# A two-layer decode step: bf16 turns of o and of row sums, a norm without helper tiles, another projection form, and a new written-out order

## The chip, the cores and the metric

The kernel runs on one core of a Trainium2 chip. A core has a matrix engine (TensorE, here PE, with its weight loads as PEld), a vector engine (DVE), a scalar engine (ACT), a general engine (POOL) and a queue engine (SP) that issues nearly all transfers. Each engine works off its own instructions in order; engines wait for each other by semaphores. Matrix products go to PSUM, eight banks of 128 partitions by 512 FP32 numbers; everything else lives in SBUF. The metric is the device time of the whole program in microseconds, lower is better.

## The reference

Four sequences (B = 4) with one token each pass through two identical layers. A layer is a windowed attention over a key/value cache and a gated feed-forward block, both with a norm ahead and a residual add behind:

```
x = x + attention(norm(x));  x = x + ffn(norm(x));  and the same once more

attention: q = x @ wq            (448 -> 16 heads of 256; 8 key/value heads, two q heads each)
           k, v = last 2048 positions of the caches, per sequence and key/value head
           p = softmax(q k^T / 16);  o = p v;  out = o @ wo      (4096 -> 448)
ffn:       (silu(x @ w_gate) * (x @ w_up)) @ w_down              (448 -> 1792 -> 448)
norm:      (x - mean) / sqrt(var + 1e-5)
```

Both layers use the same weights and the same caches. Inputs and output are bf16. A pair of one sequence and one key/value head reads 1 MB of keys and 1 MB of values; there are 32 such pairs per layer, 64 units of work in all.

## The kernel before, in words

The program is built as a graph of operations (`Graph`, `Op`), each with an engine, a short kind name and the data that it reads and writes. The order on every engine is not worked out at build time: it is written down as lists of operation numbers (`SEQ_PE`, `SEQ_DVE`, `SEQ_ACT`, `SEQ_POOL`, `SEQ_SP`), and `SLOTS` says into which of 34 SBUF units of 0.5 MB each load goes. `schedule` reads the lists and adds, for every load into a unit that is in use, a wait for the last reader of what lies there; `_place_waits` sets the semaphores. `DUR` holds estimated durations and only serves to sort the waits. Entries such as `w13` in `SEQ_PE` are fillers: products of zeros with 512 columns into bank A (`filler`, L1111–1114) that change no value and keep PE working; there are 317.

`PLAN` says in which stages the 64 units run and which are done two at a time (`+`) or with their scores one after the other (`&`). `HOLD` names the keys and values of layer 0 that stay in SBUF for layer 1. The last stages are `210+310`, `311` and `315+312`; a unit is written as sequence, layer, head.

A unit or pair of units (`group`, L831) goes through these steps. Its keys are transposed in place by DVE (L856, twice per unit). POOL spreads q over a block form `qe` (L896). PE forms the scores (L890), DVE takes the maximum (L906), PE spreads it (L911, L914), DVE negates it (L920), ACT takes the exponent (L924), PE turns the probabilities (L937), ACT copies them (L946), PE and DVE sum them (L954, L959), PE multiplies by the values (L968), and POOL inverts the sum (L981). The result o then lies in rows that have to be turned into columns. In all groups but the last this takes an ACT copy to bf16 (L995), a DVE subtraction (L997) that leaves the high and the low part of o as one bf16 tile, and two bf16 products (L1003). In the last group (`final`) ACT copies o as FP32 (L984) and two FP32 products turn it (L989). DVE scales it into `oT` (L1013).

The output projection (`out_proj`) has two forms. By rows (`opr`, L1033) four products per head add 4×448 results into rows of bank A. By columns (`opc`, L1025) sixteen products add 128-row columns into a corner of the same bank. The column form is used in the stage that ends a token's layer, the row form elsewhere. When a token's layer ends, `rows(t)` brings its row sums back to columns: ACT copies 448 FP32 numbers of bank A (L773), PE turns them with four FP32 products (L778; the trace counts two PE passes for each) and a product with zeros (`clear`, L529), and DVE adds them to x (L782). `residual` adds the column sums (L525).

`norm(t)` sums x and its square (L525, L538) on DVE, PE adds over the partitions and spreads the result (`nstat`, L541), DVE subtracts the mean (L545) and copies the sums (L547), and POOL works out the reciprocal root (L557–561). The width 448 is 3×128 + 64, so the last 64 rows of wq, gate and up are laid over 128 partitions as two half rows each. In before, row r of these lies in partitions 2r and 2r+1, and the last 64 values of x are spread to match by a PE product with a helper tile `twice` (L549) and a DVE product with a second one, `par` (L552), into spare columns of the statistics tile. `qproj` then forms q for a token (L595), scales it (L601), turns it (L611), copies it (L618) and selects head parts by sixteen products (L626). The feed-forward block has a column form (`ffn`, L720, L731, L734–747, L756) and a row form for tokens 1 and 2 of layer 0 (`ffn_row`, L657–685).

The queue order by which SP issues loads is fixed by `SEQ_SP`: first keys, x and wq, then keys and values mixed with wo, gate, up and down, and at the end two key halves and four value halves of the last group.

Of the kernel before, what the change touches and what calls it, by code (L numbers as in the profile page):

```python
# [5 lines left out]
ACT = mybir.ActivationFunctionType  # L6
# [4 lines left out]
INT32 = mybir.dt.int32  # L11
# [38 lines left out]
    "000 001 002 003 004 005 006 007 010 011 100 101 102 103 104 105 110 201 202 205 206 207 302 304 306 307 310 "  # L50
# [35 lines left out]
)  # L86
SEQ_DVE = (
# [21 lines left out]
)  # L109
SEQ_ACT = (  # L110
# [8 lines left out]
)  # L119
# [221 lines left out]
def build(nc, A_x, A_k_cache, A_v_cache, A_wq, A_wo, B_x, B_w_gate, B_w_up, B_w_down, out):  # L341
# [3 lines left out]
    with ExitStack() as es:  # L345
        def sb(name, shape, dt):
            return es.enter_context(nc.sbuf_tensor(name, shape, dt))
# [831 lines left out]
```

## Time and profile before

| | |
|---|---|
| time, median of 3 runs | 281.68 us (281.52 to 282.57) |
| the profiled execution | 281.3 us, its span 279.4 us |
| PE busy | 256.0 us (92%) |
| DVE busy | 179.5 us (64%) |
| POOL, ACT busy | 80.3 us, 61.8 us |
| read from memory | 103.91 MB, 372 GB/s over the span |
| granted PE clock, mean | 0.964 |

In what follows a row of a timeline has the start, the length, the engine, the line of the kernel, the operation and its operands (output `<-` input), and how many instructions were merged; in brackets stands how long the engine had been idle before and what it had waited for. A row of a group has the operands, the count, then the busy time of all and the mean time of one in ns, then the idle time ahead of them. A row of a stretch has the stretch, its length, and for each engine the busy time and the number of instructions, then the granted clock of PE, the share of the DMA engines and the rate. Products overlap on PE, so the mean time of one is longer than its share of a row of many.

### The profile page before, as it was taken

The page shows a single profiled execution, that of the slowest core. Times are in us where ns is not written, and L with a number is a line of the kernel's source. Part 1 is how long each engine was busy: PE and PEld are TensorE (multiplying, and loading weights), DVE is VectorE, ACT ScalarE, POOL GpSimd, SP SyncE. Part 2 cuts the span into 40 slices and gives each one's busy share as a digit, 9 for nine tenths or more (in the row PEclk, how much of TensorE's full clock was granted, in tenths as well). Part 3 has the DMA queues.
Part 4 walks back from the last instruction along what each step waited for, and adds up shares of the span by engine and source line. Part 5 has one row for each costly group of instructions (what it writes and reads, how often), then busy time and mean ns, then how long its engine had stood idle before and what let it go on. Part 6 is the DMA issues. An engine that isn't in the chain of part 4 may idle for free. (4 is left out here: it accounts for less than half of the span.)

```text
span 279.4 us, 10832 instructions
## 1 busy us (share of the span) xinstructions
PE 256.0 (92%) x4796; PEld 149.3 (53%) x4796; DVE 179.5 (64%) x548; ACT 61.8 (22%) x173; POOL 80.3 (29%) x225
## 2 busy tenths in 40 slices
PE   3899799999999999999998889999998999999995
PEld 1333344334775554545555445655764577576684
DVE  4388644634603789668766978793898858489421
ACT  0003010101113222232223123134213212423301
POOL 1033230011121534315232333243153242423430
PEclk9999989999999999999999999999999999989857
DMA  7999999999999999999999999999999999999200
GB/s 282 428 419 420 413 409 409 395 394 406 401 394 409 396 412 410 412 401 361 409 401 420 418 412 409 393 369 412 414 420 402 405 400 382 392 414 412 115 2 2
DMA packets 26894, 104.61 MB, mean 374 GB/s; under 512 B 2652, under 2 KB 6752, under 8 KB 22880
## 3 DMA queue, kind: packets, MB, share of 16 engines
q1 hardware_dynamic: 26839, 103.92, 93.5%
q8 instruction: 37, 0.61, 0.9%
q14 instruction: 10, 0.07, 0.1%
q10 hardware_dynamic: 8, 0.00, 0.0%
HBM read 103.91 MB, written 0.00 MB: 372 GB/s over the span
## 5 line engine op out<-in xcount | busy, mean ns | idle before, releaser
L856 DVE STREAM_TRANSPOSE half<-half 128x1024 uint32<-128x1024 uint32 x88 | 106.6, 1228 | 9.3 <-DMA half<-in_A_k_cache_dram 9.2
L1112 PE MATMUL A<-identb,small 128*128 128x512 bf16 x317 | 96.2, 399 | 4.4 <-DVE A L424 4.4
L981 POOL TENSOR_TENSOR small<-small 128x2 f32<-128x2 f32 (+1 forms) x48 | 38.5, 804 | 54.1 <-DVE small L959 54.1
L968 PE MATMUL Y<-half,pT 128*8 128x256 bf16 (+1 forms) x1024 | 45.7, 281 | 3.1 <-DMA half<-in_A_v_cache_dram 1.0
L890 PE MATMUL S<-half,qe 128*8 128x128 bf16 (+1 forms) x1536 | 43.5, 241 | 0.6 <-DVE half L856 0.2
L1112 PEld LDWEIGHTS A<-identb,small 128*128 128x128 bf16 x317 | 27.6, 104 | 29.9 <-issue 12.5
L890 PEld LDWEIGHTS S<-half,qe 128*8 128x8 bf16 x1536 | 30.8, 85 | 10.9 <-issue 1.6
L924 ACT ACTIVATE po<-S,small 104x128 bf16<-104x128 f32 (+1 forms) x48 | 19.3, 402 | 68.7 <-DVE small L920 66.6
L896 POOL TENSOR_TENSOR qe<-qc,tiny 128x64 bf16<-128x64 bf16 x64 | 17.9, 292 | 45.6 <-PE S L890 29.1
L997 DVE SCALAR_TENSOR_TENSOR po<-po,small,Y 128x256 bf16<-128x256 bf16 x47 | 22.0, 468 | 13.3 <-ACT po L995 13.2
L968 PEld LDWEIGHTS Y<-half,pT 128*8 128x8 bf16 (+1 forms) x1024 | 20.3, 85 | 17.6 <-issue 6.9
L995 ACT ACTIVATE po<-Y 128x256 bf16<-128x256 f32 x47 | 18.0, 383 | 48.1 <-PE Y L968 33.2
L906 DVE TENSOR_REDUCE tiny<-S 104x1 bf16<-104x128 f32 (+1 forms) x48 | 15.6, 326 | 11.5 <-PE S L890 11.2
L557 POOL TENSOR_SCALAR st<-st 128x1 f32<-128x1 f32 x16 | 4.2, 264 | 58.5 <-DVE st L547 52.5
L946 ACT ACTIVATE pT<-Y 128x64 bf16<-128x64 f32 (+1 forms) x48 | 12.2, 258 | 27.8 <-PE Y L937 27.7
L1033 PE MATMUL A<-wo_sb,oT 128*4 128x448 bf16 x188 | 16.4, 353 | 0.9 <-DVE oT L1013 0.9
L920 DVE TENSOR_REDUCE small<-S 104x1 f32<-104x32 f32 x48 | 8.6, 180 | 10.4 <-PE S L914 8.3
L1013 DVE TENSOR_TENSOR oT<-Y,small 128x4 bf16<-128x4 f32 (+1 forms) x63 | 8.9, 153 | 7.7 <-PE Y L989 4.6
L911 PE MATMUL S<-small,identb 104*104 104x32 bf16 x48 | 10.1, 210 | 3.4 <-DVE small L459 2.0
L1060 POOL MEMSET oT<- 128x16 bf16 x38 | 4.1, 111 | 29.9 <-PE A L1033 23.2
L959 DVE TENSOR_REDUCE small<-Y 128x2 f32<-128x32 f32 (+1 forms) x48 | 9.2, 191 | 5.0 <-PE Y L954 4.8
L778 PE MATMUL Z<-small,wide 128*128 128x1 f32 (+1 forms) x80 | 10.9, 249 | 0.5 <-ACT wide L773 0.5
(136 smaller groups left out, 268.0 us busy)
## 6 DMA issues: line engine op xcount, KB each, us to landing
half<-in_A_v_cache_dram SPq DMA_DIRECT2D x87, 512.0 KB, 10.6
half<-in_A_k_cache_dram SPq DMA_DIRECT2D x28, 1024.0 KB, 10.6
half<-in_A_k_cache_dram SPq DMA_DIRECT2D x32, 512.0 KB, 6.7
wo_sb<-in_A_wo_dram SPq DMA_DIRECT2D x8, 448.0 KB, 13.5
half<-in_A_wq_dram SPq DMA_DIRECT2D x3, 1024.0 KB, 12.3
wd_sb<-in_B_w_down_dram SPq DMA_DIRECT2D x1, 1568.0 KB, 20.2
wg_sb<-in_B_w_gate_dram SPq DMA_DIRECT2D x1, 1344.0 KB, 15.7
wu_sb<-in_B_w_up_dram SPq DMA_DIRECT2D x1, 1344.0 KB, 17.8
```

Source lines behind the costliest of these rows:

```text
L856: return e.transpose(a, a)
L890: last = e.matmul(Sb[s_][qd:qd + 8, 0:32 * 2 * J], lhsT=qe[q_][:, P, ce, :, :].rearrange("p a n -> p (a n)"), rhs=keys(kcs[P], J * x, J, c ...
L896: g.op(POOL, "qe", lambda e, P=P, t=t, kvh=kvh: e.tensor_tensor(qe[q_][:, P, :, :, :], qc[t][:, kvh, :, :].unsqueeze(2).broadcast_to([128, ...
L906: g.op(DVE, f"max{n}", lambda e: e.tensor_reduce(pmax[s_][0:R, :], Sb[s_][0:R, 0:N], AX.X, ALU.max), r=(f"s{s_}",), w=(f"pmax{s_}",), bank ...
L924: return e.activation(praw[0:R, 0:128 * n].rearrange("p (g r l) -> p g r l", g=2 * n, l=2), Sb[s_][0:R, 0:128 * n].rearrange("p (l g r) -> ...
L946: g.op(SCA, f"pt{n}", lambda e: e.activation(pf, Yb[p_][:, 0:PW], ACT.Copy), r=(f"yp{p_}",), w=(f"pT{pt}",), bank=(f"Y{p_}",))
L968: last = e.matmul(Yb[p_][32 * gg:32 * gg + M, 256:512], lhsT=pT[pt][:, gg, 2 * a + hv, 4 * P:4 * P + M] if n == 2 else p1[:, gg % 2, 2 * a ...
L981: g.op(POOL, f"pow{n}", lambda e: e.tensor_tensor(ri[p_][:, 0:2 * n], rs[p_][:, 0:2 * n], expo[:, 1:1 + 2 * n], op=ALU.pow), r=(f"rs{p_}", ...
L995: g.op(SCA, "oh", lambda e: e.activation(oh[:, :], Yb[p_][:, 256:512], ACT.Copy), r=(f"y{p_}",), w=("oh",), bank=(f"Y{p_}",))
L997: g.op(DVE, "oho", lambda e: e.scalar_tensor_tensor(out=oh[:, :], in0=oh[:, :], scalar=lomask[:, 0:1], in1=Yb[p_][:, 256:512], op0=ALU.mul ...
L1033: last = e.matmul(Ab[32 * k:32 * k + B, 0:D], lhsT=oT[oi][:, k % 2, k // 2, :], rhs=wo_sb[:, 4 * kvh + k, :], start=False, stop=False, ski ...
L1112: return e.matmul(Ab[:, 0:512], lhsT=zero[:, 0:1].broadcast_to([128, 128]), rhs=identb[:, :].unsqueeze(1).broadcast_to([128, 4, 128]), sta ...
```

## The change

- `rows(t)`: ACT copies the row sums as bf16, DVE subtracts that copy from the FP32 sums (a new instruction, `rowsub`) and so gets the rest as a second bf16 tile, and PE turns both with eight bf16 products after a product with zeros.
- The last group turns o like all others: ACT copy to bf16, DVE subtraction, two bf16 products. The FP32 form is gone.
- `norm` no longer uses `twice`, `par` and the PE product; two DVE instructions subtract the mean from the last 64 values and write them to the upper and the lower half of a tile `xe` of its own. The last rows of wq, gate and up are loaded to match: half h of row r goes to partition 64h + r.
- The projection of the second-last stage (`311`) is done by columns.
- The selection of q multiplies by a mask in the DVE copy and needs four products instead of sixteen; `tsel` is a view of the identity instead of a tile.
- The product with zeros (`clear`) comes first instead of last.
- All five order lists and `SLOTS` are new. The order of the loads is the same, but keys 001 and 201 (sequence, layer, head) come in two halves where they came in one piece, and keys 106 and 112 in one piece where they came in halves. There are 270 fillers for 317.

```diff
         def clear(e, out, m):
-            return e.matmul(out, lhsT=zero[:, 0:1].broadcast_to([128, 64]), rhs=identb[:, 0:m], start=False, stop=True,
-                            skip_group_check=True)
+            e.matmul(out, lhsT=zero[:, 0:1].broadcast_to([128, 64]), rhs=identb[:, 0:m], start=True, stop=False,
+                     skip_group_check=True)
...
-            vec("nxn", lambda e: e.tensor_scalar(xn[:, :, t], x[:, t, :], Z2[:, 0:1], None, op0=ALU.subtract),
+            vec("nxn", lambda e: e.tensor_scalar(xn[:, :, t], x[:, t, 0:3], Z2[:, 0:1], None, op0=ALU.subtract),
...
-            g.op(PE, "nxe", lambda e: e.matmul(Z2[:, 16:17], lhsT=twice[:, :],
-                                                    rhs=xn[:, 3, t:t + 1], start=True, stop=True, skip_group_check=True),
-                 r=(f"xn{t}", "twice"), w=("z2",), bank=("Z2",))
-            vec("nxe2", lambda e: e.tensor_tensor(xe[:, :, t], par[:, :], Z2[:, 16:17].broadcast_to([128, 2]), op=ALU.mult),
-                ("z2", "par"), (f"xe{t}",), ("Z2",))
+            for h in range(2):
+                vec(f"nx{1 + h}", lambda e, h=h: e.tensor_scalar(
+                    xe[64 * h:64 * h + 64, h, t:t + 1], x[64:128, t, 3:4], Z2[64:128, 0:1], None, op0=ALU.subtract),
+                    (f"x{t}", "z2"), (f"xe{t}",), ("Z2",))
...
         def rows(t):
-            g.op(SCA, "rowcp", lambda e: e.activation(wide[:, 0:D], Ab[:, 0:D], ACT.Copy), r=(f"row{t}",), w=WIDE, bank=("A",))
+            g.op(SCA, "rowcp", lambda e: e.activation(wideb[:, 0:D], Ab[:, 0:D], ACT.Copy), r=(f"row{t}",), w=("wa",), bank=("A",))
+            vec("rowsub", lambda e: e.tensor_tensor(wideb[:, 512:512 + D], Ab[:, 0:D], wideb[:, 0:D], op=ALU.subtract),
+                (f"row{t}", "wa"), ("wb",), ("A",))
             def turn(e):
-                for cc in range(4):
-                    q = 64 * (cc // 3)
-                    e.matmul(Zb[q:128, cc:cc + 1], lhsT=wide[:, 128 * cc:128 * cc + 128 - q], rhs=rmask[:, t:t + 1],
-                             start=(cc == 0), stop=True, skip_group_check=True)
-                return clear(e, Zb[0:64, 3:4], 1)
+                clear(e, Zb[0:64, 3:4], 1)
+                for c0 in (0, 512):
+                    for cc in range(4):
+                        q = 64 * (cc // 3)
+                        c = c0 + 128 * cc
+                        last = e.matmul(Zb[q:128, cc:cc + 1], lhsT=wideb[:, c:c + 128 - q], rhs=rsel[:, t:t + 1],
+                                        start=(c == 0), stop=(c0 > 0), skip_group_check=True)
+                return last
...
-            if final:
-                g.op(SCA, "ohf", lambda e: e.activation(ohf[:, :], Yb[p_][:, 256:512], ACT.Copy), r=(f"y{p_}",),
-                     w=("oh", "praw"), bank=(f"Y{p_}",))
...
-                out_proj(oi, ts, kvh, bool(full))
+                out_proj(oi, ts, kvh, bool(full) or si + 2 == len(plan()))
...
-        load(1 << 19, wq_sb[:, 3 * 4096:], A_wq[384:448, :].rearrange("r (h c) -> (r h) c", h=2), "wq3", 4096)
+        load(1 << 19, wq_sb[:, 3 * 4096:], A_wq[384:448, :].rearrange("r (h c) -> h r c", h=2), "wq3", 4096)
```

More of the change, by code (lines that the diff above doesn't have):

```diff
@@ L355, in build @@
         identb = sb("identb", [128, 128], BF16)
-        twice = sb("twice", [128, 128], BF16)
-        tiny = sb("tiny", [128, 16 + NS], BF16)
+        rep32 = sb("rep32", [128, 32], BF16)
+        tiny = sb("tiny", [128, 14 + NS], BF16)
         onesb, qmask, osel, rsel = tiny[:, 0:1], tiny[:, 2:6], tiny[:, 6:10], tiny[:, 10:14]
-        par = tiny[:, 14:16]
-        pmax = [tiny[:, 16 + s:17 + s] for s in range(NS)]
-        tsel = sb("tsel", [128, 4, B], BF16)
+        pmax = [tiny[:, 14 + s:15 + s] for s in range(NS)]
+        tsel = identb[:, :].rearrange("p (j x) -> p j x", j=4)[:, :, 0:B]
         selt = [sb(f"selt{h}", [128, 4, 12], BF16) for h in range(2)]
@@ L432, in build @@
         for a in range(4):
[L433 removed]
+            g.op(DVE, "d1", lambda e, a=a: e.memset(qmask[32 * a:32 * a + 32, a:a + 1], DH ** -0.25), r=("qmask",),
                  w=(f"qmask{a}",))
@@ L484, in build @@
                 r=("identb",), w=("osel",))
-            g.op(DVE, "d1", lambda e, P=P: e.tensor_reduce(
-                oself[:, 2 * P:2 * P + 2], iv[:, :, 0, P, 0, :].rearrange("p j n -> p n j"), AX.X, ALU.max),
-                r=("identb",), w=("oself",))
         il = identb[:, :].rearrange("p (k y n) -> p k y n", y=2, n=2)
@@ L616, in qproj @@
                 kw = dict(acc=("z",)) if b else dict(w=("z",))
-                g.op(PE, "qturn", lambda e, b=b: turn(e, b), r=(WIDE[b], "tsel"), bank=("Z",), **kw)
-            vec("qs", lambda e: e.tensor_copy(qS[:, 0:32 * n], Zb[:, 0:32 * n]), ("z",), ("wa",), ("Z",))
-            def select(e):
-                last = None
-                src = qS[:, 0:32 * n].rearrange("p (k x) -> p k x", x=4)
-                for c in range(4):
-                    for a in range(4):
-                        o = Z2[32 * a:32 * a + 32, 0:128 * n].rearrange("p (k c x) -> p k c x", c=4, x=4)[:, :, c, :]
-                        last = e.matmul(o, lhsT=identb[:, 32 * c:32 * c + 32], rhs=src, start=(c == 0), stop=(c == 3),
-                                        skip_group_check=True)
+                g.op(PE, "qturn", lambda e, b=b: turn(e, b), r=(WIDE[b], "identb"), bank=("Z",), **kw)
+            vec("qs", lambda e: e.tensor_tensor(
+                qS[:, 0:128 * n].rearrange("p (k c x) -> p k c x", c=4, x=4),
+                Zb[:, 0:32 * n].rearrange("p (k x) -> p k x", x=4).unsqueeze(2).broadcast_to([128, 8 * n, 4, 4]),
+                qmask[:, :].unsqueeze(1).unsqueeze(3).broadcast_to([128, 8 * n, 4, 4]), op=ALU.mult),
+                ("z",) + tuple(f"qmask{a}" for a in range(4)), ("wa",), ("Z",))
+            def select(e):
+                for a in range(4):
+                    last = e.matmul(Z2[32 * a:32 * a + 32, 0:128 * n], lhsT=rep32[:, :], rhs=qS[:, 0:128 * n], start=True,
+                                    stop=True, skip_group_check=True)
                 return last
-            g.op(PE, "qsel", select, r=("wa", "identb"), w=("z2",), bank=("Z2",))
+            g.op(PE, "qsel", select, r=("wa", "rep32"), w=("z2",), bank=("Z2",))
             for i, t in enumerate(ts):
@@ L673, in turn @@
                     last = e.matmul(Zb[:, 16 * c:16 * c + 16].rearrange("p (j t) -> p j t", j=4),
-                                    lhsT=wideb[:, 128 * c:128 * c + 128], rhs=tsel[:, :, :], start=(c == 0), stop=True,
+                                    lhsT=wideb[:, 128 * c:128 * c + 128], rhs=tsel, start=(c == 0), stop=True,
                                     skip_group_check=True)
                 return last
-            g.op(PE, "fturn", turn, r=WIDE + ("tsel",), w=("z",), bank=("Z",))
+            g.op(PE, "fturn", turn, r=WIDE + ("identb",), w=("z",), bank=("Z",))
             vec("fht", lambda e: e.tensor_copy(hT[:, :], Zb[:, 0:64]), ("z",), ("wb",), ("Z",))
@@ L799, in x_in @@
         def x_in(e):
+            clear(e, Zb[0:64, 12:16], 4)
             for cc in range(4):
                 q = 64 * (cc // 3)
-                e.matmul(Zb[q:128, 4 * cc:4 * cc + 4], lhsT=xio[0:B, 128 * cc:128 * cc + 128 - q], rhs=identb[0:B, 0:B],
+                last = e.matmul(Zb[q:128, 4 * cc:4 * cc + 4], lhsT=xio[0:B, 128 * cc:128 * cc + 128 - q], rhs=identb[0:B, 0:B],
                          start=(cc == 0), stop=(cc == 3), skip_group_check=True)
-            return clear(e, Zb[0:64, 12:16], 4)
+            return last
         g.op(PE, "xin", x_in, r=xio_k + ("identb", "zero"), w=("z",), bank=("Z",))
-        g.op(DVE, "d1", lambda e: e.tensor_copy(xs[:, :, :], Zb[:, 0:16].rearrange("p (c t) -> p t c", t=B)),
+        g.op(DVE, "xcp", lambda e: e.tensor_copy(xs[:, :, :], Zb[:, 0:16].rearrange("p (c t) -> p t c", t=B)),
              r=("z",), w=tuple(f"xs{t}" for t in range(B)) + tuple(f"x{t}" for t in range(B)), bank=("Z",))
@@ L982, in group @@
                 ri[p_][:, 0:2 * n], rs[p_][:, 0:2 * n], expo[:, 1:1 + 2 * n], op=ALU.pow), r=(f"rs{p_}", "expo"), w=(f"ri{p_}",))
-            if final:
-                g.op(SCA, "ohf", lambda e: e.activation(ohf[:, :], Yb[p_][:, 256:512], ACT.Copy), r=(f"y{p_}",),
-                     w=("oh", "praw"), bank=(f"Y{p_}",))
-                def flipf(e):
-                    for dh in range(2):
-                        last = e.matmul(Yb[p_][:, 2 * n * dh:2 * n * dh + 2 * n],
-                                        lhsT=ohf.rearrange("p (m e) -> p e m", e=2)[:, dh, :], rhs=oself[:, 0:2 * n],
-                                        start=dh == 0, stop=dh == 1, skip_group_check=True)
-                    return last
-                g.op(PE, "flipf", flipf, r=("oh", "praw", "oself"), w=(f"yp{p_}",), bank=(f"Y{p_}",))
-            else:
-                g.op(SCA, "oh", lambda e: e.activation(oh[:, :], Yb[p_][:, 256:512], ACT.Copy), r=(f"y{p_}",),
-                     w=("oh",), bank=(f"Y{p_}",))
-                g.op(DVE, "oho", lambda e: e.scalar_tensor_tensor(
-                    out=oh[:, :], in0=oh[:, :], scalar=lomask[:, 0:1], in1=Yb[p_][:, 256:512], op0=ALU.mult,
-                    op1=ALU.subtract), r=(f"y{p_}", "oh", "lomask"), w=("oh",), bank=(f"Y{p_}",))
-                def flip(e):
-                    for dh in range(2):
-                        last = e.matmul(Yb[p_][:, 2 * n * dh:2 * n * dh + 2 * n],
-                                        lhsT=oh[:, :].rearrange("p (m e) -> p e m", e=2)[:, dh, :],
-                                        rhs=osel[:, 0:2 * n], start=dh == 0, stop=dh == 1, skip_group_check=True)
-                    return last
-                g.op(PE, "flip", flip, r=("oh", "osel"), w=(f"yp{p_}",), bank=(f"Y{p_}",))
@@ new lines, in group, with flip @@
+            g.op(SCA, "oh", lambda e: e.activation(oh[:, :], Yb[p_][:, 256:512], ACT.Copy), r=(f"y{p_}",),
+                 w=("oh",), bank=(f"Y{p_}",))
+            g.op(DVE, "oho", lambda e: e.scalar_tensor_tensor(
+                out=oh[:, :], in0=oh[:, :], scalar=lomask[:, 0:1], in1=Yb[p_][:, 256:512], op0=ALU.mult,
+                op1=ALU.subtract), r=(f"y{p_}", "oh", "lomask"), w=("oh",), bank=(f"Y{p_}",))
+            def flip(e):
+                for dh in range(2):
+                    last = e.matmul(Yb[p_][:, 2 * n * dh:2 * n * dh + 2 * n],
+                                    lhsT=oh[:, :].rearrange("p (m e) -> p e m", e=2)[:, dh, :],
+                                    rhs=osel[:, 0:2 * n], start=dh == 0, stop=dh == 1, skip_group_check=True)
+                return last
@@ L1068, in build @@
                     members.append((pos, t, layer, kvh))
-                group(gi, members, outs, split, pos + 1 == len(seq))
+                group(gi, members, outs, split)
                 gi += 1
```

50 lines of the change are left out of this document (22 added, 28 removed), and 161 rows, old and new, of tables (SEQ_ACT, SEQ_DVE, SEQ_PE, SEQ_POOL).

## The prediction

> **What bounds the kernel now.** I read the page's slices first, then stretches of time by engine, then the order of work at the end. The slices:
>
> ```profile
> span 279.4 us, 10832 instructions
> ...
> PEclk9999989999999999999999999999999999989857
> DMA  7999999999999999999999999999999999999200
> ```
>
> The transfers keep the DMA engines busy to the 38th slice of 6.99 us; what follows is a tail without them. The stretches show both phases:
>
> ```profile
> 120.00:136.00 16.00, 14.89 (x280) 8.65 (x278) 13.00 (x33) 4.52 (x14) 4.81 (x14) 1.00 1.01 383
> 178.00:190.00 12.00, 11.24 (x247) 7.01 (x248) 10.35 (x35) 3.08 (x9) 4.73 (x14) 1.00 0.99 379
> 202.00:224.00 22.00, 20.42 (x443) 11.78 (x443) 18.45 (x50) 5.78 (x17) 8.55 (x26) 1.00 1.02 409
> 228.00:240.00 12.00, 11.68 (x270) 8.35 (x270) 8.23 (x28) 2.27 (x7) 4.83 (x13) 1.00 0.99 381
> ...
> 260.00:263.00 3.00, 2.44 (x54) 1.51 (x42) 2.08 (x13) 1.19 (x3) 0.93 (x2) 1.00 0.15 60
> ```
>
> Columns: stretch, length, busy time and (x) instructions of PE, weight load, DVE, ACT, POOL, then clock, DMA share, GB/s. Outside the feed-forward bursts the stream runs at 409 GB/s; in the three bursts it falls to 383, 379 and 381. At 409 these would be shorter by 16×(1−383/409) + 12×(1−379/409) + 12×(1−381/409) = 1.0+0.9+0.8 = 2.7 us: all that faster engines could win there. PE is busy 93, 94 and 97% of them, DVE 81, 86 and 69%. At 260–263 the share is 0.15: the stream is over at about 260.5. The queue's own timeline shows what it ends with:
>
> ```profile
> 243.03 0.91 SPq L850 DMA_DIRECT2D half<-in_A_k_cache_dram  x2
> 243.99 3.63 SPq L866 DMA_DIRECT2D half<-in_A_v_cache_dram  x4
> ```
>
> Two key halves and four value halves of 0.52 MB take 1.28 us each at 409 GB/s, so the last key half comes about 4×1.28 = 5 us before the end of the stream, near 255.5 to 257 (an estimate). Now the timeline of the end:
>
> ```profile
> 256.30 2.36 DVE L856 STREAM_TRANSPOSE half<-half 128x1024 uint32<-128x1024 uint32 x2
> ...
> 257.02 0.55 ACT L773 ACTIVATE wide<-A 128x448 f32<-128x448 f32 x1 [0.30 <-PE A L1033]
> ...
> 257.07 0.83 PE L968 MATMUL Y<-half,pT 128*8 128x256 bf16 x24
> ...
> 258.81 1.12 PE L890 MATMUL S<-half,qe 128*8 128x256 bf16 x32
> ...
> 260.31 0.20 PE L1003 MATMUL Y<-tiny,po 128*128 128x4 bf16 x2
> ...
> 260.77 0.67 PE L1025 MATMUL A<-oT,wo_sb 128*128 128x2 bf16 x16
> ...
> 262.80 0.22 DVE L959 TENSOR_REDUCE small<-Y 128x4 f32<-128x64 f32 x1
> ...
> 262.83 0.43 PE L1033 MATMUL A<-wo_sb,oT 128*4 128x448 bf16 x4
> ...
> 263.07 1.90 PE L968 MATMUL Y<-half,pT 128*8 128x256 bf16 x32
> ...
> 264.90 1.64 PE L778 MATMUL Z<-small,wide 128*128 128x1 f32 x7
> ...
> 265.01 0.38 ACT L984 ACTIVATE po<-Y 128x256 f32<-128x256 f32 x1 [1.16 <-PE Y L968]
> ...
> 266.57 1.01 PE L989 MATMUL Y<-small,po 128*128 128x4 f32 x4
> ...
> 267.44 0.56 PE L541 MATMUL Z<-st,small 128*128 128x2 f32 x2
> 267.62 0.24 DVE L1013 TENSOR_TENSOR oT<-Y,small 128x4 bf16<-128x4 f32 x2 [4.60 <-PE Y L989]
> ...
> 267.87 1.47 PE L1025 MATMUL A<-oT,wo_sb 128*128 128x1 bf16 x32
> ...
> 269.38 0.16 DVE L525 SCALAR_TENSOR_TENSOR xr<-xr,A 128x4 f32<-128x4 f32 x1 [1.04 <-PE A L1025]
> ```
>
> The last two key transpositions end at 258.66, the last scores start 0.15 later, the last P·V runs 263.07 to 264.97, and the residual add begins at 269.38: 4.41 us between, in which PE works off the FP32 row turn and then the FP32 turn of o one after the other. That is where this change bites hardest.
>
> **The change, part by part.** The groups that price it:
>
> ```profile
> L1112 PE MATMUL A<-identb,small 128*128 128x512 bf16 x317 | 96.2, 399 | 4.4 <-DVE A L424 4.4
> ...
> L997 DVE SCALAR_TENSOR_TENSOR po<-po,small,Y 128x256 bf16<-128x256 bf16 x47 | 22.0, 468 | 13.3 <-ACT po L995 13.2
> ...
> L778 PE MATMUL Z<-small,wide 128*128 128x1 f32 x60 | 8.8, 261 | 0.5 <-ACT wide L773 0.5
> ...
> L549 PE MATMUL Z<-xn,twice 128*128 128x1 bf16 x16 | 2.8, 176 | 0.6 <-issue 0.4
> ...
> L667 DVE SCALAR_TENSOR_TENSOR wide<-wide,small,Z 128x512 bf16<-128x512 f32 x2 | 1.5, 748 | 0.2
> ```
>
> *Row subtraction (new, ten times, on DVE).* No row shows it. Over 448 elements from PSUM it costs 448/512×748 = 0.65 us by L667, 448/256×468 = 0.82 by L997. I take 0.66, as L667 is nearer in length. It waits for ACT's copy (0.55), and every transposition behind it waits too; on PE the row turn now waits for DVE, with scores and P·V queued behind it. For token 2 of layer 1 the new order puts it between the last two transpositions. The first of them ended near 256.30+1.18 = 257.48, the copy at 257.57; the projection ahead of that copy now comes before a P·V, so the copy may end some 0.2 earlier. The last transposition, the last scores and all behind them then move by +0.7 (+0.3 if the first transposition starts earlier, +0.9 with the dearer row and the copy where it is).
>
> *Second-last projection by columns.* Sixteen matmuls (0.67) in place of four (0.43) ahead of the last P·V, which waited for the sum that ends at 263.02 anyway: they begin near 262.6 and end near 263.27, so +0.2 (0 to +0.3). The row copy still follows them, and copy and subtraction (0.55+0.66) end near 264.5, under the P·V.
>
> *Last P·V to residual add.* On PE after the P·V now: one statistics product (0.56), a filler (0.40), the row turn of nine bf16 matmuls, the turn of o. Nine at the price of the column projection (1.47/32 = 46 ns) are 0.41, sum 1.37. On DVE beside it: copy 0.38, subtraction of o 0.47, two gaps of 0.05: 0.95, covered by PE's 1.37. Then turn 0.20, scaling 0.24, projection 1.47, gaps 0.12: 3.40 in place of 4.41, −1.0. If PE's three steps all fit under DVE's 0.95, it is −1.4. If the nine matmuls cost what the FP32 ones do (1.64/7 = 234 ns), PE's part is 3.07 and the gap 5.10: +0.7. I stay with 46 ns, since L1025 is a bf16 product of the same shape.
>
> *Norm without helpers.* PE loses 16 helper products (176 ns each), DVE gets 16 more additions of about 0.15. At the end the first gate product started 0.05 after the helper product, so −0.05. Gate and up read the last rows from a tile of their own:
>
> ```profile
> 228.81 1.20 PE L720 MATMUL Z<-xn,wg_sb 128*128 128x32 bf16 x42
> ...
> 229.96 0.57 PE L720 MATMUL Z<-st,wg_sb 128*128 128x64 bf16 x7
> ```
>
> Seven of the strided form take 81 ns each, 42 of the other 29 ns; at the latter price with twice the columns (58 ns) one group wins 0.16. Only the gate's is on the path: 0 to −0.16, I take −0.1.
>
> *Clock.* Of 3.4 us windows:
>
> ```profile
> 242.50:245.90 3.40, 3.20 (x100) 2.33 (x100) 2.36 (x5) 0.38 (x1) 1.80 (x6) 1.00 1.04 428
> 245.90:249.30 3.40, 3.29 (x70) 2.85 (x73) 2.46 (x15) 1.50 (x4) 0.25 (x2) 1.00 0.99 411
> 249.30:252.70 3.40, 3.40 (x88) 2.60 (x84) 3.40 (x4) 0.38 (x1) 1.68 (x5) 0.51 1.02 414
> ...
> 259.60:263.00 3.40, 2.84 (x66) 1.90 (x58) 2.08 (x13) 1.19 (x3) 0.93 (x2) 1.00 0.25 96
> 263.00:266.40 3.40, 3.40 (x45) 2.52 (x41) 0.02 (x1) 0.93 (x2) 1.90 (x4) 0.50 0.02 5
> ```
>
> [...] The tail of the new order has five fillers between the last scores and the gate product, the old one two, and no run of 1-column FP32 passes. The last P·V took 1.90 at half clock and would take 0.83×32/24 = 1.11 at full: 0 to −0.8, I take the middle, −0.4, as the placing of the windows decides.
>
> The Trainium skill ("TensorE: Matmul & The Clock Gate", section "Part 1: The HAM clock gate") says that a free-running window of 3413 ns decides the next one's clock by PE's activity. The trace agrees: its half-clock stretches are 249.3–252.7 and from 263.0 on. By that rule alone five fillers promise nothing for the tail: with this term at 0 the sum below would be −0.55, by the rows it is −0.95. [...]
>
> *The stream.* Order and bytes of the loads are the same; two key loads come in halves and two in one piece that did not before. PE loses 47 fillers (96.2/317 = 0.30 us each, 14 in all) and, at each of nine earlier row turns, eight matmuls of 8.8/60 = 147 ns for nine of 46: 1.18−0.41 = 0.77 us; DVE gets nine subtractions and the additions, 9×0.66+16×0.15 = 8.3 us over 260. PE was the fuller engine in each burst, so I take −0.3, between −2.7 (all dips gone) and +2.6 (four subtractions, those of 122, 135, 174 and 186 us, in full on the path). The last rows of wq, gate and up keep bytes and row length: 0, covered by the stream, which they leave unchanged; a dearer load would cost its full time there. The query's selection (4 matmuls for 16, a wider DVE copy that may cost 0.1 each of five times if uncovered) and four constants fewer: 0, hidden beside the transfers.
>
> Sum: +0.7+0.2−1.0−0.05−0.1−0.4−0.3 = −0.95 us. The profiled execution took 281.3 us (its span 279.4), 0.4 under the median of 281.68; I apply the sum to the median: 280.7.
>
> **The rivals.** *A, the stream gains:* with PE relieved all three bursts run at 409 GB/s: 281.7−0.65 (the tail's terms) −2.7 = 278.3. For it: PE 93 to 97% busy in the bursts; against: waits there pass from PE to ACT and DVE and back, and DVE gets longer. [...] *C, the subtraction stalls DVE* (the end on the other side by one mechanism): in the four places named it stands ahead of transpositions while the queue waits: 281.7−0.65+2.6 = 283.7; it decides once more than one is on the path. *D, nothing shows:* the subtraction eats what the turns give back: 281.7.
>
> **How the numbers follow.** My forecast (with D) 0.48, A 0.22, B 0.14, C 0.16. The likeliest case alone runs from 279.7 to 282.0. Leaving out 1 in 10 on each side, the range is 277.9 to 284.0. About 0.5% (1.4 us) is what a measurement can tell from no change: faster means under 280.3, slower over 283.1. Faster: 0.21 of A and 0.15 of the forecast, 0.36; slower: 0.28 of the 0.30 of B and C, as B with one window stays under; same: the rest, 0.36.
>
> **What would show it.** Right: the gap from last P·V to residual add near 3.4 us; a subtraction near 0.66 between the last two transpositions; row turns near 0.4; bursts still near 380 GB/s. Wrong: half-clock windows between 60 and 240 us (B), DVE idle ahead of the subtraction with the queue waiting (C), bursts at 409 GB/s (A), or a stream that ends more than 1 us from 260.5.

## The result and the profile after

The changed kernel takes 315.78 us (median of 6 runs, 311.48 to 320.37), the one before on the same chip 281.69. The ratio is 1.111 (95% interval 1.106 to 1.117): 11% slower, where 280.7 us was forecast and 284.0 was the upper end. Here and below a ratio is that of undisturbed runs to undisturbed runs of the kernel before on the same chip, whose median lay between 281.7 and 284.0 us from chip to chip; kernels are therefore compared by ratio, and a length is read from one execution.

The slices of the changed kernel's page (its profiled execution took 311.48 us, one slice is 7.74 us):

```profile
span 309.5 us, 10634 instructions
...
PEclk9977599998679999989999999999999999997997
DMA  7999995396999979999999999999999997999600
GB/s 295 428 313 280 358 411 238 142 327 251 315 399 364 318 267 329 420 411 412 330 346 411 411 413 413 411 381 340 374 420 412 408 407 284 367 421 406 277 2 5
```

The last of these lines in before, with slices of 6.99 us:

```profile
GB/s 282 428 419 420 413 409 409 395 394 406 401 394 409 396 412 410 412 401 361 409 401 420 418 412 409 393 369 412 414 420 402 405 400 382 392 414 412 115 2 2
```

There the rate stays between 361 and 428 GB/s from the second slice to the 37th. Here the third to fifth fall to 313, 280 and 358, then come holes at 238 and 142 and a ragged stretch to the sixteenth. The later dips (330, 340, 284) stand singly. The stretches of that early part (columns as in the prediction):

```profile
21.00:35.00 14.00, 2.68 (x16) 1.05 (x14) 1.94 (x5) 1.28 (x1) 1.90 (x7) 0.74 1.02 282
35.00:45.00 10.00, 7.76 (x66) 2.75 (x66) 5.20 (x10) 1.37 (x2) 1.05 (x4) 0.85 1.02 411
62.00:68.00 6.00, 6.00 (x61) 2.28 (x53) 1.50 (x7) 1.36 (x4) 0.29 (x1) 1.00 0.95 311
68.00:80.00 12.00, 6.22 (x46) 2.22 (x47) 4.62 (x4) 0.43 (x2) 0.00 (x0) 0.82 0.78 288
80.00:86.00 6.00, 4.74 (x84) 2.07 (x83) 2.62 (x9) 0.54 (x2) 1.87 (x4) 0.79 1.02 308
```

From 21 to 35 us PE works 2.7 of 14 us, and yet the DMA share is 1.02 with only 282 GB/s: the DMA engines count as busy, but move two thirds of what they move elsewhere. Two shorter stretches (62–68, 80–86) look the same, at 311 and 308 GB/s; between them the share itself falls to 0.78. What PE and DVE wait for (waits: total, times, longest; then DVE's group of key transpositions, which idled 9.3 us in before):

```profile
PE Z L581 <- DMA half<-in_A_wq_dram: 11.3, 1, 11.3
PE Y L961 <- DMA half<-in_A_v_cache_dram: 7.1, 5, 5.8
```

```profile
L849 DVE STREAM_TRANSPOSE half<-half 128x1024 uint32<-128x1024 uint32 x88 | 107.0, 1229 | 27.4 <-DMA half<-in_A_k_cache_dram 27.2
```

One wait of 11.3 us is for wq, the rest for keys and values behind it. The three slow stretches are the three loads whose row order changed. The trace records each addition to a load's semaphore, here called a landing event; a load of 128 rows has sixteen, and the kernel waits for the full count. By the last event of each, the last rows of wq landed at 34.69, the load ahead at 18.79, a gap of 15.90 us where before shows 18.74 to 19.97, 1.23. The rows of up came 5.75 us and those of gate 6.1 us after the load ahead, for 0.22 MB, which at 409 GB/s is 0.56. In excess that is 14.7+5.2+5.5 = 25.4 us.

Not all of the stream stood still. Of the value load queued behind wq's last rows fourteen events came at 18.86 to 20.77, about as in before (sixteen at 20.11 to 21.24), and two at 34.53 and 35.72, each some 1.1 us behind one of wq's late events. So a later load was complete only when its last two shares had come. The queue also issued later: its issue of that value load stood for 9.99 us in place of 0.47 (before, then after), for a reason that the profile does not show.

```profile
4.64 0.47 SPq L866 DMA_DIRECT2D half<-in_A_v_cache_dram  x1
```

```profile
4.83 9.99 SPq L859 DMA_DIRECT2D half<-in_A_v_cache_dram  x1
```

### The profile page after: what moved, and what is told of

Read it like the earlier page. It is cut to its first block, busy times and chain, and to the rows that moved or that the text cites. A ratio compares the mean times of both kernels' runs of the same rounds, so it can differ in the third digit from the quotient of the medians.

```text
span 309.5 us, 10634 instructions
## 1 busy us (share of the span) xinstructions
PE 249.5 (81%) x4683; PEld 140.9 (46%) x4683; DVE 193.2 (62%) x571; ACT 62.7 (20%) x173; POOL 80.3 (26%) x225
## 4 chain that ended last, share of the span: by engine, by line
PE 38%; DMA 23%; DVE 17%; SPq 15%; issue 3%; ACT 3%; POOL 1%; DVEq 0%; ACTq 0%
DMA half<-in_A_v_cache_dram 14%; SPq L859 10%; PE A L1093 9%; DVE half L849 9%; PE S L883 6%; PE Y L961 6%; DMA half<-in_A_k_cache_dram 4%; DMA wo_sb<-in_A_wo_dram 4%; SPq L837 3%; PE A L1006 2%; PE Z L706 2%; PE A L1014 2%; DVE po L978 2%; SPq L487 2%; PE Y L930 2%
## 5 line engine op out<-in xcount | busy, mean ns | idle before, releaser
L1093 PE MATMUL A<-identb,small 128*128 128x512 bf16 x270 | 82.6, 403 | 5.0 <-DVE A L420 4.5
L883 PE MATMUL S<-half,qe 128*8 128x128 bf16 (+1 forms) x1536 | 44.7, 245 | 2.5 <-POOL qe L889 1.2
L1093 PEld LDWEIGHTS A<-identb,small 128*128 128x128 bf16 x270 | 24.2, 104 | 31.4 <-issue 14.6
L961 PEld LDWEIGHTS Y<-half,pT 128*8 128x8 bf16 (+1 forms) x1024 | 19.6, 84 | 23.2 <-DMA half<-in_A_v_cache_dram 8.6
L581 PE MATMUL Z<-half,xe 128*4 128x512 bf16 x40 | 4.1, 399 | 11.9 <-DMA half<-in_A_wq_dram 11.3
```

Source lines behind the costliest of these rows:

```text
L883: last = e.matmul(Sb[s_][qd:qd + 8, 0:32 * 2 * J], lhsT=qe[q_][:, P, ce, :, :].rearrange("p a n -> p (a n)"), rhs=keys(kcs[P], J * x, J, c ...
L961: last = e.matmul(Yb[p_][32 * gg:32 * gg + M, 256:512], lhsT=pT[pt][:, gg, 2 * a + hv, 4 * P:4 * P + M] if n == 2 else p1[:, gg % 2, 2 * a ...
L1093: return e.matmul(Ab[:, 0:512], lhsT=zero[:, 0:1].broadcast_to([128, 128]), rhs=identb[:, :].unsqueeze(1).broadcast_to([128, 4, 128]), sta ...
```

## The experiments

The loads come first, then the rest of the change, then its tail.

**The loads.** `e1_two_parts`: each of the three loads as two transfers, one for each half h.

```diff
-        load(1 << 19, wq_sb[:, 3 * 4096:], A_wq[384:448, :].rearrange("r (h c) -> h r c", h=2), "wq3", 4096)
+        load2(1 << 19, wq_sb[:, 3 * 4096:], A_wq[384:448, :].rearrange("r (h c) -> h r c", h=2), "wq3", 4096)
...
+                e.dma_start(dst[0:64, :], src[0]).then_inc(dsems[sem], 16)
+                return e.dma_start(dst[64:128, :], src[1])
```

> The changed kernel, but each of the three loads of the last rows (wq, up, gate) is issued as two transfers of 64 whole rows, one per half, to the same places; all else as changed. Theory L (the new row order makes these three transfers run on a few DMA engines only: their landings come 15.9, 5.8 and 6.1 us after the transfer before them): the time falls by about 26 us and more, to 277.5 to 281.5. Rival O (the loss comes from the new written-out order, fewer fillers or the row subtraction): it stays above 300.

Measured: 293.67 us, ratio 1.042 (1.033 to 1.050). The loads are the largest part, but neither theory's range holds the time: some 11 us stay.

`e2_wq_narrow`: as e1, with wq's rows in one transfer again.

> The changed kernel with gate and up in two parts, wq's last rows in one transfer as changed. Theory L: the time of e1_two_parts plus what wq's last rows cost alone, 15.9 - 1.3 = 14.6 us, so 292 to 296. Rival O: the same as e1_two_parts, above 300.

Measured: 304.29 us, ratio 1.081 (1.075 to 1.087). Theory L's range, reckoned from a faster e1, is missed. wq's load alone costs 10.6 us over e1, where L had 14.6, and those of gate and up the 8.6 us by which the changed kernel's ratio lies above that (0.0305 of 282).

`e3_before_loads`: the kernel before with the three loads of the change.

```diff
-.rearrange("r (h c) -> (r h) c", h=2)
+.rearrange("r (h c) -> h r c", h=2)
```

> The kernel before with nothing changed but the row order of the three loads (half h of row r to partition 64h + r). The last 64 rows of wq, gate and up then lie in other partitions than its norm spreads x over, so the products of the last 64 values are not the reference's. Theory L: 281.7 + 26 to 32 = 304 to 314. Rival O: no change, 281 to 283.

Measured: 308.84 us, ratio 1.092 (1.081 to 1.103), as theory L had it. wq's rows land 15.6 us after the load ahead, and PE comes to a stop in a stretch in which it is busy in before (first before, then e3):

```profile
26.00:32.00 6.00, 5.07 (x97) 2.85 (x93) 3.58 (x9) 0.45 (x1) 1.56 (x7) 1.00 1.00 407
```

```profile
26.00:32.00 6.00, 0.00 (x0) 0.00 (x0) 0.00 (x0) 0.00 (x0) 0.00 (x0) 0.50 1.01 261
```

`k4_wq_four` and `k8_wq_eight` ask why. Only wq's last load is rewritten, with a slowest source dimension of 4 or 8 (the outermost one of the access pattern; in `h r c` it is h, which counts 2):

```diff
-A_wq[384:448, :].rearrange("r (h c) -> (r h) c", h=2)
+A_wq[384:448, :].rearrange("r (h c) -> (r h) c", h=2).rearrange("(i a) c -> a i c", a=4)
```

> The kernel before with one load rewritten: the last rows of wq are read with a slowest source dimension of 4 (every fourth half row first), same bytes and row length; the values meet other rows than in the reference. In the changed kernel the same load with a slowest dimension of 2 landed 15.9 us after the load ahead of it, in before 1.3. If the number of DMA engines that work on a load is the slowest dimension (2 there), 4 engines do it in half the time: landing about 7 to 8 us after the one ahead, 3 + 2 = 5 landing events, and the time is 285 to 288 us. If any reordering of the rows costs the same: 14 to 16 us gap, 291 to 295 us.

> As k4_wq_four with a slowest source dimension of 8: by the number of engines, landing about 3.5 to 4.5 us after the load ahead, 282.5 to 285 us. If any reordering of the rows costs the same: 14 to 16 us gap, 291 to 295 us.

Measured: 291.72 us, ratio 1.031 (1.016 to 1.046), and 288.75 us, 1.022 (1.010 to 1.034). Landings of this load in four traces:

```
kernel    slowest source dimension   landing events   load ahead   this load   gap us   next value load: events early + late
before    128 (one piece)            16               18.74        19.97        1.23    16 + 0
k8         8                          9               19.05        24.89        5.84     8 + 8
k4         4                          5               19.63        28.86        9.23    12 + 4
after      2                          3               18.79        34.69       15.90    14 + 2
```

For 2, 4 and 8 the events are the slowest dimension n plus one, and of the next value load just n events come late: in k8 eight at 20.28 to 20.99 and eight at 25.42 to 25.93, in k4 twelve at 19.57 to 20.38 and four at 28.63 to 29.85. So n engines share the load, and the others go on. The gap falls with n: from 2 to 4 by 6.67, from 4 to 8 by 3.39, half of that. A gap of 2.5 + 26.8/n fits these three (not the 1.23 of before, where it would give 4.2). By this fit each engine takes 0.52 MB/26.8 us = 19.6 GB/s, an estimate, where sixteen at 409 GB/s do 25.6 each. This is what the Trainium skill says ("DMA: Bandwidth & Descriptors", section "Why a DMA increments its semaphore by 16 and not by 1"): a transfer runs on the largest number of engines up to 16 that divides the slowest dimension of both sides, and the sequencer adds the missing counts at once. The trace agrees: with 2 engines, one event 1.1 us after the issue and two more at the landing. The 2.5 us that do not scale stay unexplained; the rows of up and gate, 0.115 MB for each of two engines, took 5.75 and 6.1 us, which 19.6 GB/s gives without them (5.9). That any reordering of rows costs the same is excluded. Gaps and times came out above the ranges expected: 8.8 and 6.2 us over before by the ratios, for 8.0 and 4.6 us of gap in excess. The intervals are wide, but no part of the gaps is seen to be hidden.

**The rest of the change.** `e4_loads_back`: the changed kernel with the three loads of before.

```diff
-.rearrange("r (h c) -> h r c", h=2)
+.rearrange("r (h c) -> (r h) c", h=2)
```

> The changed kernel with only the row order of the three loads put back (half h of row r to partition 2r + h, as before), everything else of the change kept; the last 64 values of x then meet other rows of wq, gate and up than in the reference, so the values differ, not the work. With the same loads in two parts the kernel took 293.67 us, 11.4 above its kernel before (282.24). Theory L (the loads alone are dear, the two-part form too: its six landings are some 6 us later in sum than the whole loads of before, and what stands behind them follows): all of it goes, the stream ends near 260 to 263 us, the shorter tail (-2.3) shows, 278.5 to 281.5 us. Rival O (new order, fewer fillers, or the row subtractions on DVE starve the stream): 286 to 291 us, the stream ends 6 to 10 us later than in the kernel before, with idle time of the queue between 80 and 260 us.

Measured: 288.30 us, ratio 1.024 (1.017 to 1.032). The loads are worth 0.087 of 282, 24.5 us, near their 25.4 us of gaps; e1 is some 5 us slower, and by its landings most of that is its half transfers: wq's last rows are in at 22.13 where e4 has 20.07, those of gate at 65.72 where e4 has 61.99. What stays is 2.4%, some 7 us, and it is rival O's: the last key transposition ends at 267.33, in before at 258.66. Its slices:

```profile
PEclk9979999999999999997999999779999999997997
DMA  7999999999999999999999999989999999999600
GB/s 286 425 409 420 419 413 406 393 393 406 396 403 346 352 417 413 409 398 372 360 345 410 416 406 413 366 285 381 370 410 421 405 406 347 341 418 410 246 2 3
```

The first twelve slices are close to those of before. From the thirteenth on come dips to 346, 345, 285 and 341, the deepest beside a half-clock stretch (181.9 to 188.7).

`e5_fillers`: as e4, with 31 entries `w4` and 16 entries `w10` of the PE list doubled.

> As e4_loads_back, with 47 more fillers (31 entries w4 and 16 entries w10 doubled), so 317 as in the kernel before. If the fewer fillers cost time by the clock (rival B of the prediction), this is 2 to 5 us faster than e4_loads_back and shows fewer half-clock windows between 60 and 240 us. If they cost nothing, it is within 1 us of e4_loads_back or up to 4 us slower, since 47 fillers are 14 us more of PE work.

Measured: 298.43 us, ratio 1.057 (1.046 to 1.068). Against e4 the ratio is 3.2% higher. In the two profiled executions the mean clock is 0.961 and 0.969, but over all runs that the ratios rest on it is 0.964 in e4 and 0.962 in e5: no clock was won in the mean, and more fillers at these places are work in the way. In the deepest dip PE is nearly full:

```profile
85.00:90.00 5.00, 5.00 (x86) 3.10 (x83) 0.54 (x7) 0.37 (x2) 0.00 (x0) 1.00 0.83 328
90.00:95.00 5.00, 4.76 (x75) 1.97 (x75) 2.10 (x8) 2.36 (x5) 1.99 (x5) 1.00 0.73 228
```

`e6_no_rowsub`: as e4, the subtraction cut to one column.

```diff
-wideb[:, 512:512 + D], Ab[:, 0:D], wideb[:, 0:D], op=ALU.subtract)
+wideb[:, 512:513], Ab[:, 0:1], wideb[:, 0:1], op=ALU.subtract)
```

> As e4_loads_back, with the row subtraction cut to one of its 448 columns and the low half of the row turn multiplied by zeros: the low part of the row sums is left out, the instructions and their order stay. If the ten subtractions (0.6 us each) lie on the path only once, at the end, this is 0.3 to 0.8 us faster than e4_loads_back; if they stall the stream on DVE (rival C), it is 2 to 6 us faster.

Measured: 287.49 us, ratio 1.013 (1.002 to 1.024). Against e4 the medians differ by 0.8 us, the ratios by 1.1%, and the intervals overlap: inconclusive. The profiled execution of e6 also has no half-clock window between 60 and 240 us, where that of e4 has three.

`e10_row_turns_only` puts the ten bf16 row turns into the kernel before (the body of `rows` as in the diff above; each subtraction where DVE is estimated free behind ACT's copy). `e14_row_turns_cut` is the same with the cut of e6.

> The kernel before with one part of the change: all ten row turns as bf16 with the subtraction on DVE, order and loads as before. Rival C of the prediction and rival P here (a subtraction that stalls DVE starves the stream): 283.5 to 287 us. If only the last one is on the path: 281 to 282.5 us, since it saves PE about 1 us there and adds up to 0.7 on DVE.

> As e10_row_turns_only, which took 289.96 us, with the subtraction cut to one of its 448 columns and the low half of the turn multiplied by zeros (the low part of the row sums is left out; instructions and order stay). In e10_row_turns_only PE waited 8.3 us on these ten subtractions. If their length (0.6 us) is the cost: 282 to 285.5 us. If it is the wait for DVE itself, whatever is ahead of it there: 287 to 290 us.

Measured: 289.96 us, ratio 1.032 (1.024 to 1.039), and 287.29 us, 1.010 (0.996 to 1.025). One part that looked like 0.7 us costs 3% in the places chosen here, more than either expectation; a lower granted clock goes with it (0.947 to 0.955, where before had 0.957 to 0.990 on that chip). The waits of PE show how (before, then e10):

```profile
PE Z L778 <- ACT wide L773: 0.5, 2, 0.3
```

```profile
PE Z L778 <- DVE wide L774: 6.9, 7, 2.0
```

The FP32 turn waited for ACT only; the bf16 turn waits for DVE, which has other work ahead, and PE stands for up to 2.0 us with scores and P·V queued behind it. With the subtraction cut this wait falls from 6.9 to 4.1 us; that the time falls with it is likely (1.032 to 1.010) but not settled, as the intervals just touch. The new order softens the wait; in e4 it falls on the product with zeros ahead of the turn:

```profile
PE Z L517 <- DVE wide L761: 1.9, 6, 0.7
```

`e13_norm_only`: the kernel before with the norm's two DVE subtractions.

> The kernel before with one part of the change: the norm without helper tiles, two DVE subtractions in the place of the PE helper product and the DVE product; loads, order and all else as before (the values differ, since the rows of wq, gate and up stay where they were). The two took 227 ns each in the changed kernel where 150 were forecast, 24 of them. If they are hidden beside the stream, as the prediction has it: 281 to 282.5 us. If they stall the statistics product behind them on PE (2.1 us of waiting in e4_loads_back): 283.5 to 286 us.

Measured: 284.74 us, ratio 1.007 (1.002 to 1.011): some 1.8 us, so 283.5 from a kernel before of 281.7, the lower edge of the second expectation. Its groups, and those of e4 for comparison:

```profile
L550 DVE TENSOR_SCALAR xe<-xr,Z 64x1 bf16<-64x1 f32 x24 | 5.4, 227 | 0.7
L550 DVE TENSOR_SCALAR xe<-xs,Z 64x1 bf16<-64x1 f32 x8 | 1.8, 226 | 0.2
```

```profile
L761 DVE TENSOR_TENSOR wide<-A,wide 128x448 bf16<-128x448 f32 x10 | 6.2, 619 | 3.3 <-ACT wide L760 3.3
L537 DVE TENSOR_SCALAR xe<-xr,Z 64x1 bf16<-64x1 f32 x24 | 5.4, 227 | 0.7
```

Two runs cross the order with the parts. `e7_new_parts_old_order` has e4's instructions in the order of before, `e8_old_parts_new_order` the instructions of before in the new order (lists and `SLOTS` carried over operation by operation; the few without a counterpart stand where their engine is estimated free).

> All of the changed kernel's instructions, with the row order of the three loads put back (the values differ from the reference's for that reason alone), but in the order of the kernel before: its five lists and SLOTS carried over, 317 fillers, the same keys whole or in halves; the row subtraction stands where DVE is first free behind ACT's copy. Theory N (the new order costs the 5.7 us that e4_loads_back had over its kernel before; the parts themselves are good for the tail): 279 to 281.5 us. Rival P (the parts cost it, above all the ten row subtractions on DVE, whatever the order): 285 to 289 us.

> The instructions of the kernel before in the changed kernel's order (lists, SLOTS, 270 fillers, keys whole or in halves as there); the helper product of each norm stands where PE is first free behind its input. Theory N: the stream starves as in e4_loads_back and the short tail is missing, 285 to 291 us. Rival P: 281 to 284 us.

Measured: 295.18 us, ratio 1.053 (1.042 to 1.063), and 292.78 us, 1.042 (1.033 to 1.052). Both crossings are slower than both matched kernels (1.000 and 1.024). Theory N falls with e7 and rival P with e8, and the shares of order and parts do not add. A likely reason, not shown, is that a written-out order fits the durations it was made for; the operations placed by estimate may cost time too, and e7's granted clock (0.930 to 0.938) is below that of e4 (0.960 to 0.969).

**The tail.** `e9_tail_only`: the kernel before with the bf16 turn of o in the last group, the second-last projection by columns, and the bf16 row turn for the last token. `e11_flip_and_columns`: the first two alone.

```diff
-                group(gi, members, outs, split, pos + 1 == len(seq))
+                group(gi, members, outs, split, False)
...
-                out_proj(oi, ts, kvh, bool(full))
+                out_proj(oi, ts, kvh, bool(full) or si + 2 == len(plan()))
```

> The kernel before with three parts of the change at its end alone: o of the last group turned as bf16, the second-last projection by columns, and the bf16 row turn with its subtraction for the last token only; order and loads as before. The last P.V to residual add took 4.41 us before and 3.08 in the changed kernel, and the end from the last key transposition on 20.74 and 18.47. If this gain belongs to these parts and needs neither the new order nor the new norm: 279.5 to 280.7 us. If it is the clock that the new order's tail keeps up: 281 to 282.5 us.

> The kernel before with two parts of the change at its end alone: o of the last group turned as bf16 and the second-last projection by columns; row turns, loads and order as before, so no row subtraction anywhere. e9_tail_only, which has the bf16 row turn of the last token besides, was not to be told from before (ratio 0.9942 to 1.0069), though its last key transposition to its end took 19.29 us in place of 20.74. If the tail's gain is real and only hidden by the scatter of both: 0.2 to 0.6% under before. If the gain needs the bf16 row turn, or is eaten ahead of the tail: within 0.2% of before, or above it.

Measured: 282.56 us, ratio 1.0005 (0.994 to 1.007), and 283.46 us, 1.003 (0.997 to 1.009). No gain is seen, though e9's interval leaves room for 1.4 us. The changed kernel does show the shorter tail that was forecast (timeline of after):

```profile
295.50 1.05 PE L961 MATMUL Y<-half,pT 128*8 128x256 bf16 x32
...
296.18 0.62 DVE L761 TENSOR_TENSOR wide<-A,wide 128x448 bf16<-128x448 f32 x1 [0.59 <-ACT wide L760]
...
297.30 0.63 PE L770 MATMUL Z<-tiny,wide 128*128 128x1 bf16 x8
...
297.86 0.20 PE L984 MATMUL Y<-tiny,po 128*128 128x4 bf16 x2
...
299.63 0.16 DVE L513 SCALAR_TENSOR_TENSOR xr<-xr,A 128x4 f32<-128x4 f32 x1 [1.17 <-PE A L1006]
```

From the end of the P·V to the residual add are 3.08 us, in before 4.41. But e3, with the old FP32 turns, has this:

```profile
293.04 1.05 PE L968 MATMUL Y<-half,pT 128*8 128x256 bf16 x32
...
294.02 0.98 PE L778 MATMUL Z<-small,wide 128*128 128x1 f32 x7
...
294.98 0.63 PE L989 MATMUL Y<-small,po 128*128 128x4 f32 x4
...
297.19 0.16 DVE L525 SCALAR_TENSOR_TENSOR xr<-xr,A 128x4 f32<-128x4 f32 x1 [1.01 <-PE A L1025]
```

3.10 us: the P·V takes 1.05 there too, and the FP32 turns 0.98 and 0.63 where before took 1.64 and 1.01. They ran at full clock, by where the window fell. In e9 the P·V fell into a half-clock window (its profiled execution took 288.32 us; only lengths inside its tail are read):

```profile
271.68 1.83 PE L985 MATMUL Y<-half,pT 128*8 128x256 bf16 x32
...
276.52 0.16 DVE L525 SCALAR_TENSOR_TENSOR xr<-xr,A 128x4 f32<-128x4 f32 x1 [1.03 <-PE A L1042]
```

Here the new parts take 276.52−273.51 = 3.01 us. The stretches from the end of the P·V to the residual add have the clock beside them (before, after, e3, e9):

```profile
264.97:269.38 4.41, 4.41 (x48) 4.32 (x48) 0.59 (x6) 0.38 (x1) 0.87 (x4) 0.50 0.00 0
```

```profile
296.55:299.63 3.08, 3.02 (x47) 2.19 (x47) 1.47 (x8) 0.38 (x1) 0.97 (x4) 1.00 0.00 0
```

```profile
294.09:297.19 3.10, 3.06 (x48) 2.86 (x48) 0.52 (x6) 0.38 (x1) 1.61 (x6) 1.00 0.00 0
```

```profile
273.51:276.52 3.01, 2.78 (x48) 2.58 (x46) 1.07 (x6) 0.38 (x1) 0.76 (x3) 0.50 0.00 0
```

So by one execution of each, the new parts win 1.40 us over before when the window is at half clock and next to nothing at full clock.

## Why the prediction was wrong, by its own steps

- *The last rows of wq, gate and up (0, "which they leave unchanged").* This step failed. Bytes and row length are unchanged, but the access pattern's slowest dimension went from 128 to 2, so the load ran on 2 engines of 16, and every load behind it had to wait for its own shares on these two. In place of 0: 25.4 us of gaps, 24.5 us in the time by e4 and some 26 by e3. That "a dearer load would cost its full time there" held.
- *Row subtraction (+0.7).* The length was right (0.66 forecast, 0.62 in the mean), and it stands between the last two key transpositions as said (after):

```profile
288.12 1.25 DVE L849 STREAM_TRANSPOSE half<-half 128x1024 uint32<-128x1024 uint32 x1 [0.43 <-DMA half<-in_A_k_cache_dram]
...
289.29 0.58 DVE L761 TENSOR_TENSOR wide<-A,wide 128x448 bf16<-128x448 f32 x1
...
289.80 1.23 DVE L849 STREAM_TRANSPOSE half<-half 128x1024 uint32<-128x1024 uint32 x1
```

  The nine others were put under the cover of the stream; that is where the step fell short. PE waits for them, and in the old order the ten cost 3% (e10). The mechanism was written down, "on PE the row turn now waits for DVE, with scores and P·V queued behind it", but priced for DVE alone: rival C has 2.6 us for four on the path, where e10 shows 6.9 us of PE waiting in seven.
- *Last P·V to residual add (−1.0), and the clock (−0.4).* 3.40 forecast, 3.08 measured; P·V 1.11 forecast at full clock, 1.05 measured. That they came so close is in part luck: the 3.40 took the statistics product and the projection at half-clock prices (0.56, 1.47), and after had them at full clock (0.38, 1.27). But the two terms are largely one: at full clock the FP32 turns leave the gap no longer (3.10 in e3). The rows 1.64 and 1.01 had been measured at half clock and were taken for the price of the operation. That the P·V met full clock in after was a matter of where the window fell; e9, with the same turns, met half. What decides a window's clock is not shown: before also has half clock at 34.3 to 37.7, and neither the count of products nor PE's busy time tells it. The window at 245.9 holds 70 products in 3.29 us and is followed by half clock, this one holds fewer and is followed by full clock:

```profile
239.10:242.52 3.42, 2.79 (x60) 1.28 (x52) 1.10 (x6) 2.52 (x5) 0.29 (x2) 1.00 0.98 370
```

  In the time no gain is shown (e9, e11).
- *Second-last projection (+0.2).* Sixteen products took 0.66, where 0.67 was forecast; the term is too small to be seen apart.
- *Norm (−0.15 with the tile of its own).* Each of its DVE instructions takes 0.227 us and not 0.15, there are 32 (24 and 8) in place of 16, and the part alone costs 0.65% (0.2 to 1.1).
- *The stream (−0.3).* PE's 14 us of fillers less came out as idle time, not as rate: in e4 PE is busy 247.5 us of 285.9 (before 256.0 of 279.4), and dips at 285 to 346 GB/s stay. The busy share of PE in the bursts counted fillers, which move no data.
- *Rival B (fewer fillers, lower clock in mid-stream).* Its sign shows: e4 has half clock at 130.7 to 134.1 and 181.9 to 188.7, before has none between 37.7 and 249.3. But e11, with the order and the fillers of before up to its tail, has one such window too (189.8 to 193.2) and no loss, and with 47 fillers more only 200.6 to 204.0 is left and the time rises (e5). So fillers at these places do not win it back; what the windows cost e4 is not shown.
- *The other rivals.* Rival A is gone with e4, whose stream is slower, not faster. Rival C named the right instruction, but priced a delay of DVE; what e10 shows is PE's wait for DVE, and more of it. D, that nothing shows, is what the tail alone gives (e9, e11).

Open is how the 2.4% of e4 divide between the new order, the clock and the parts: e6 does not decide it, and e7 and e8 show that it may not divide at all. No version tried here beats the kernel before.

## What to carry to other kernels

Read a load's access pattern from its outermost dimension, not from its bytes and row length: one `h r c` in place of `(r h) c` made the same 0.52 MB land 15.9 us behind the load ahead in place of 1.2. A count of landing events below 16 gives it away, and so do loads behind it of which a few events come late. A product's price read in a half-clock window is not the operation's price; look for the same row at full clock before costing its removal. In a kernel with a written-out order, a new operand from a busier engine is priced by the wait it puts on the engine that needs it, not by its own length.

## What was not expected of the hardware

The slowest source dimension set the number of engines for a load (3, 5, 9 and 16 landing events, gaps of 15.90, 9.23, 5.84 and 1.23 us). The engines that had no part in it went on, and yet the loads queued behind it were complete only after it: of the next value load of e3 fourteen events came at 18.82 to 20.34 and two at 34.27 and 35.35, with the narrow load landing at 34.31. The lag lasts: of the load of the down weights, issued at 86.33 in after, fourteen events are in by 101.94 and the last two come at 105.27 and 106.67. During the narrow load the profile's DMA share stayed at 1.01 to 1.02 with 261 to 282 GB/s moved, so that only the rate shows it, not the busy share.
